# Two of seven column pairs by plain matmuls, and a new written order of steps

## The chip, the core and the metric

The kernel runs on one core of one Trainium2 chip. The core has a matrix engine (PE, with weight loads shown apart as PEld), a vector engine (DVE), a scalar engine (ACT), a general engine (POOL) and a queue engine (SP) that issues all transfers here. The metric is the device time of one execution in microseconds; lower is better.

## The reference

An input x of 2048 tokens by 512 is normalised by rows, and the result goes through two branches that are added to x. A is linear attention with 32 heads of 16 and a learned feature map; B is a gated unit without a nonlinearity.

```python
xn = _layernorm(x)
# A
qkv = (xn @ wqkv).reshape(B, S, 3, H, Dh)            # H = 32, Dh = 16
phi = [softmax(p @ w_phi), softmax(-p @ w_phi)]      # for q and for k, over the last axis
kv  = sum over tokens of phi_k * v;  z = sum over tokens of phi_k
o   = (phi_q @ kv) / (phi_q . z + 1e-6);  A = o @ wo
# B
B = ((xn @ w_gate) * (xn @ w_up)) @ w_down           # w_gate, w_up: 512 x 1792
out = x + A + B
```

## The kernel before

Tokens come in 16 tiles of 128, in four groups of four. Group 0 (tokens 0 to 511) is normalised at the start and transposed by PE. The other groups are normalised by steps s, sc and a, and transposed by a transfer on SP (step xt, line 523); group 1 (tokens 512 to 1023) lies in the tile x4, groups 2 and 3 in x16, as f16.

The gate and up product of group 0 is plain: for each of the 14 blocks of 128 columns a step g (4 matmuls of 512 columns with w_gate, line 351), a copy gc to SBUF, a step u (the same with w_up) and a step h, the product of both on DVE (line 371). For groups 1 to 3 the weights are scaled by a power of two in place (steps up, line 359), and columns k and k+7 form a pair, k from 0 to 6. A pair is multiplied with seven products of half-size blocks in place of eight (block_steps, from line 802): steps p1 to p7, 2 matmuls each, for gate (even b) and up (odd b), where b = 2k or 2k+1. Sums of weights (steps t) and of tokens (steps z for groups 2 and 3, Nz for group 1) are their inputs. Keeps k1 to k3 on ACT, joins j2, j7, j3 on DVE, a direct copy or product d, and for up the multiplications m on POOL or DVE make the hidden tile hT out of them. Groups 2 and 3 use matmuls of 512 columns. Group 1 has the same steps with an N in front and matmuls of 256 columns, with accumulators of its own (pool ps_f) that exist between the marks =f and =ab2 of the list.

The attention: steps vk or k (projection), kx and ky (exponentials, ACT), kr and ki (sum and reciprocal, DVE), kp (POOL, line 559) and kv (PE, sum over tokens, two accumulators that are masked by kvm0 and kvm1 at the end). For queries q, qx, qy, qr, qi, qp likewise, then the transposing transfer qt (line 616), ab (PE, line 627, one buffer of accumulators), de, rd, ot (DVE) and the transposing transfer oT (line 660). The folded weights come from steps fk and fq (line 471); fq waits for the transposing load wq.

The way out: for groups 0 and 1 and token tiles 8 and 12 steps f (w_down and wo, line 678), fs, and the store fo. Tiles 9 to 11 with 13 to 15 form three pairs n and m = n + 4, with seven products of half blocks again (pair_steps, steps P, K, A, B, J; sums S of hidden blocks and ct, cb, wt of w_down), and each tile's row is stored by one step X (line 1015).

The order of all this is written out as one list of words (ORDER): every word is a step, with /a, /v or /g for ACT, DVE or POOL where a step can run on more than one. Each engine runs its words in the order of the list; a second table (SLOTS) says which buffer of its ring each tile takes, six PSUM banks among them. Where a step with both inputs in SBUF goes to DVE, the next POOL step of the list is made to wait until it is over:

```python
        if on_pool and turn is not None:
            tc.add_manual_dep(on_pool[0], turn.name, AFTER, reason="turns")
            turn = None
        if on_dve and both_in_sbuf.match(name):
            turn = on_dve[-1]
```

Of the kernel before, what the change touches and what calls it, by code (L numbers as in the profile page):

```python
# [30 lines left out]
fqa0/v vk6.1 ky6 kv1 g2 fq2 kv2 kx6 kr4 ki4 kr6 ki6 fqv0/a fqv2/a kp4/g u5 kv3 vk7.0 vk7.1 kr5 kp6/g vc6/a gc2/a
n1.3 fqa2/a ky7 vk8.0 vk8.1 kv4 kx7 ki5 h5 u2 kr7 ki7 n1.4 kp5/g vc8/a kx8 ky8 a12/a vk10.0 vk10.1 vc7/a ky10
kx10 a13/a kp7/g h2 vk9.0 kv5 kr8 ki8 kp8/g kv6 xt12 vk9.1 ky9 vc10/a kx9 n0.4 q0.0 q0.1 a15/v kr10 vk11.0
vk11.1 ky11 ki10 kx11 kv7 kv8 vk12.0 q1.0 q1.1 kp10/g xt13 a14/v kr9 ki9 kp9/g vc11/a vc9/a xt14 Nz0/v qy0 qx0
kr11 ki11 qr0 qi0 g8 gc8/a qy1 u10 qx1 kp11/g n0.0 kv9 vk13.0 vk12.1 kv10 qr1 h10 xt15 ky12 kx12 qp0/g qi1
# [5 lines left out]
f2.6 f0.3 f2.5 f0.5 f1.1 qp3/g ot0 qx4 qy4 ab2 f1.8 qr4 up41/a qy7 qx7 qp6/g de2 qi4 f1.7 rd2 fs1 ot2 qt3 oT0
qp4/g q9.0 f3.5 q9.1 q8.0 q8.1 f0.2 qr7 z1/g inv0 ab3 qt6 oT2 up21/a de3 qi7 rd3 f3.3 ot3 qx9 qt4 t00/v t02/v
Nz1/v f0.8 up20/a qy9 qp7/g p1.1 f0.7 p1.0 qx8 qy8 k1.1/a Nz3/g k1.0/a ab5 de5/a up11/a f0.6 p2.0 f0.0 t01/v
p6.0 k2.0/a rd5 ot5 n2.5 up60/a f2.7 ab6 t03/g j2.0 f2.8 p7.0 de6/v k3.0/a oT3 f3.8 fs0 rd6 ot6 p2.1 p6.1 oT5
qt7 oT6 fs2 ab4 j2.1 fo2 z3/g de4/a rd4 ot4 k2.1/a q13.0 q13.1 qr8 p5.0 up10/a j7.0 t10/g Nz2/g p4.0 d4.0/a p7.1
Np2.1 ab7 de7/a f3.6 p5.1 f3.7 k3.1/a rd7 ot7 qy13 p4.1 p3.0 =f fs3 Np1.1 up31/a Nk1.1/a Np1.0 Nk1.0/a p2.3
Np6.1 qx13 j3.0 Np6.0 p2.2 Nj2.1 Nk2.1/a j7.1 d4.1 Nk2.0/a up30/a t11/g m2.1/g Np2.0 Nj2.0 t12/g p3.1 j3.1 Np7.0
Np7.1 Nk3.1/a Nk3.0/a p1.2 k1.2/a p1.3 qr9 m7.1/g Np4.1 Np4.0 Nd4.0/a p5.2 t13/v Np5.0 up40/a Nd4.1 p6.2 Nj7.0
Np5.1 j2.2 Np3.0 k2.2/a p5.3 m3.1/g t20/g k1.3/a Nj3.0 Nj7.1 j2.3 Nm2.1/g p7.2 Np2.2 k3.2/a Np1.2 Nk1.2/a p6.3
Np3.1 t21/g p4.2 Np6.2 j7.2 p3.2 p1.4 Nj3.1 k2.3/a Nj2.2 Nm3.1/v t22/v m2.3/g S0.0/g Nk2.2/a d4.2/a k1.4/a Np7.2  # L50
Nk3.2/a j3.2 p2.4 j2.4 p7.3 Np5.2 Np4.2 p2.5 p2.6 k3.3/a Nd4.2/a qi8 j7.3 n2.0 qp8/g Nj7.2 Nm7.1/g p1.5 Np1.3
Nk1.3/a qr13 p3.3 Np3.2 k1.5/a Nj3.2 Np6.3 p6.4 p6.5 Nk2.3/a Np7.3 j2.5 m2.5/g k2.4/a m7.3/v j3.3 Np5.3 Nk3.3/a
up50/a Nj7.3 p7.4 Np2.3 Np4.3 Nd4.3 p5.4 Np3.3 Nm7.3/g Nj2.3 k3.4/a Np1.4 Nk1.4/a p4.3 j7.4 Np2.4 Np6.4 k2.5/a
t23/g Nj3.3 qi13 t30/g Nm2.3/g Nk2.4/a p3.4 j3.4 p7.5 Np7.4 Np1.5 Nj2.4 n2.1 p4.4 d4.3 Nm3.3/v Nk3.4/a t31/v
Np2.5 q10.0 Np4.4 m3.3/g k3.5/a Nk1.5/a p5.5 p4.5 Np6.5 Nj2.5 qi9 j7.5 Nm2.5/g t32/g d4.4/a Nd4.4/a Np5.4 Nj7.4
p1.6 Nk2.5/a Np7.5 Nk3.5/a q10.1 t33/v d4.5 Np3.4 wr2 Nj3.4 wf2 k1.6/a p3.5 Np4.5 up51/a Nd4.5 p6.6 Np1.6
Nk1.6/a Np2.6 qx10 j2.6 k2.6/a qp9/g j3.5 Np5.5 Nj7.5 m7.5/v m3.5/v t40/v t41/g q12.0 p5.6 Np6.6 q12.1 p7.6
Nk2.6/a Np3.5 Np7.6 Nj2.6 Nj3.5 qy10 wp2 qp13/g k3.6/a p1.7 p1.8 Nk3.6/a qx12 k1.7/a Np5.6 Np4.6 p2.7 j7.6 p3.6
p4.6 Nm7.5/g Nd4.6/a oT4 qr10 Nj7.6 Np1.7 qy12 p2.8 p6.7 Np3.6 k1.8/a Nk1.7/a j3.6 k2.7/a Np6.7 j2.7 Nk2.7/a
d4.6/a q14.0 q14.1 Np7.7 Nj3.6 j2.8 Np2.7 p7.7 Nk3.7/a qx14 Np2.9 Nm3.5/v m2.7/v t42/v Nj2.7 k3.7/a Np4.7 qy14  # L60
Np5.7 Nd4.7 p5.7 Nj7.7 t43/g Np2.8 Np1.8 p4.7 Np3.7 j7.7 Nm2.7/g Nm7.7/v Nj3.7 Nm3.7/v Nk1.8/a Np6.8 Nk2.8/a
p1.9 d4.7 p3.7 k1.9/a Np7.8 Np5.8 p6.8 m7.7/g qt13 fo3 qt8 j3.7 p2.9 Nk3.8/a Np4.8 Nd4.8/a k2.8/a p1.10 Nj7.8
Nj2.8 Np3.8 m3.7/g Np1.9 j2.9 Nk1.9/a k1.10/a t50/v ws2 Nj3.8 S1.0/g p6.9 p2.10 Nj2.9 j2.10 Np6.9 p7.8 Np5.9
p5.8 k2.9/a m2.9/v p7.9 Nk2.9/a t52/v k3.8/a j7.8 Np7.9 Nk3.9/a t51/g p5.9 p1.11 p4.8 Nj7.9 p3.8 k3.9/a p4.9
t53/g p6.10 Np4.9 Np3.9 Nm2.9/v j7.9 d4.8/a j3.8 m7.9/g qi10 k1.11/a Nd4.9 p6.11 p3.9 Nj3.9 up61/a t60/v d4.9
Nm7.9/g qp10/g k2.10/a Np1.11 p2.11 j3.9 p7.10 k2.11/a k3.10/a j2.11 Np1.10 p5.10 j7.10 Nm3.9/g m2.11/g m3.9/v
Np2.10 Np2.11 Nk1.10/a Nj2.10 p4.10 p7.11 k3.11/a q15.0 q15.1 S0.3/v qy15 Nk1.11/a d4.10/v p4.11 p3.10 p5.11
Np6.10 qx15 Nk2.10/a p1.12 Nj2.11 Nm2.11/g j3.10 Np6.11 j7.11 t61/g t62/g t63/g Np2.12 Np7.10 p2.12 f6.3 d4.11
m7.11/g k1.12/a oT7 j2.12 Nk3.10/a Np4.10 Nk2.11/a Nd4.10/a f6.1 p3.11 f6.4 qr12 Np7.11 Np5.10 p1.13 ct2.2/a
Nk3.11/a Nj7.10 j3.11 p6.12 fo1 Np3.10 k2.12/a f7.0 Np4.11 k1.13/a p2.13 Nj3.10 S0.5/v j2.13 f7.4 Np1.12 f7.1  # L70
p7.12 cb11.1/a p6.13 Nk1.12/v Nd4.11 Np5.11 f6.8 qi12 Nj7.11 Nj2.12 S1.3/g S2.4/g m3.11/v k3.12/a S0.4/g S1.4/g
Np6.12 q11.0 f6.7 Nk2.12/a ct2.1/a Np7.12 Np3.11 p5.12 qr14 Nj3.11 Nk3.12/a j7.12 Nm3.11/g qp12/g Np4.12 p4.12
Np1.13 q11.1 p3.12 d4.12/a Nd4.12/a m2.13/v Nk1.13/a Np2.13 f7.2 Np5.12 f6.2 Np6.13 f7.8 k2.13/a qr15 j3.12
p7.13 Nj2.13 Nk2.13/a ct1.0/a qi14 Nj7.12 inv1 cb11.0/v qx11 k3.13/a p5.13 Np7.13 f4.2 f4.5 Np3.12 f4.1 Nk3.13/a
p4.13 wt1.0/v Nm2.13/v Nj3.12 Nm7.11/v Np5.13 f7.7 f6.0 qt9 Np4.13 j7.13 qp14/g Nj7.13 Np3.13 d4.13 Nd4.13 p3.13
f4.3 Nj3.13 =ab2 ab8 qy11 ct2.3/g S0.1/v de8/v rd8 ot8 qi15 f4.7 f6.5 f5.2 Nm3.13/g f4.4 f5.0 ct2.0/g ab9 f7.5
S0.2/v Nm7.13/v S2.6/g de9/a rd9 ot9 S2.2/v S2.3/v F12.3 f6.6 f4.8 F12.1 f7.6 wt2.0/v S1.1/g S1.5/g qt14 qt10
qp15/g qt12 m7.13/v oT8 f4.0 j3.13 f7.3 f4.6 F12.2 f5.8 fs4 fs6 ab14 f5.7 de14/a ct1.1/a rd14 oT9 fo0 ot14
S0.6/v m3.13/v f5.1 f5.4 qr11 qi11 f8.8 oT14 f12.5 F12.6 f8.3 fs7 f5.5 f5.3 F12.5 f12.2 ab12 f8.2 P1b.10 de12/a
wt1.1/g wt2.2/g P1a.10 f5.6 f8.7 cb21.0/a f8.5 f8.4 F12.0 K1.10/v S2.1/v rd12 ot12 f12.6 qt15 fo6 P1a.11 f12.1  # L80
# [1030 lines left out]
```

## Time and profile before

| | us |
|---|---|
| median of 3 runs | 214.34 (214.32 to 215.28) |
| profiled execution | 215.05 |
| its span, first to last instruction | 213.3 |
| PE busy | 206.5 (97%), 1452 matmuls |
| DVE busy | 185.3 (87%) |
| ACT busy | 153.2 (72%) |
| POOL busy | 149.8 (70%) |
| share of the chain that ended last | PE 78%, DMA 9%, DVE 6% |
| mean granted clock of PE | 0.998 |

The span covers the instructions; the time of an execution has 1.7 us more around it. Busy PE time is a union of matmuls whose ends are modelled, so the distance between starts says more of a matmul's price than its length. A wait line reads: who waited, for what, us in total, times, longest.

### The profile page before, as it was taken

How to read it: one execution, taken by the hardware profiler on the slowest of the kernel's cores; microseconds unless marked ns; L12 is line 12 of the kernel's file. 1: busy time of each engine (PE TensorE's matmuls, PEld its weight loads, DVE VectorE, ACT ScalarE, POOL GpSimd, SP SyncE). 2: the span in 40 equal slices, each digit the busy share in tenths (PEclk: the TensorE clock that was granted, in tenths of full speed). 3: DMA queues.
4: the chain of work that ended last, by engine and by line, in shares of the span. 5: the costliest groups of instructions: out<-in, count | busy, mean ns of one | idle time of the engine just before them, and what ended most of it. 6: DMA issues, size and time to landing. Idle time of an engine off the chain costs nothing.

```text
span 213.3 us, 4174 instructions
## 1 busy us (share of the span) xinstructions
PE 206.5 (97%) x1452; PEld 117.8 (55%) x1452; DVE 185.3 (87%) x372; ACT 153.2 (72%) x296; POOL 149.8 (70%) x146
## 2 busy tenths in 40 slices
...
GB/s 158 260 274 383 379 297 177 92 8 33 70 25 77 0 68 105 147 103 77 0 3 0 0 3 32 179 13 3 0 0 0 0 130 119 101 148 75 50 78 74
DMA packets 47253, 19.95 MB, mean 94 GB/s; under 512 B 37504, under 2 KB 46976, under 8 KB 47104
## 3 DMA queue, kind: packets, MB, share of 16 engines
q1 hardware_dynamic: 47232, 19.69, 40.6%
...
HBM read 8.67 MB, written 2.10 MB: 50 GB/s over the span
## 4 chain that ended last, share of the span: by engine, by line
PE 78%; DMA 9%; DVE 6%; SPq 2%; ACT 1%; POOL 1%; issue 1%; DVEq 0%; ACTq 0%; POOLq 0%
PE sa L824 16%; PE fin L678 15%; PE sc L824 9%; PE k L337 5%; PE q L337 5%; PE da L960 5%; PE pv L337 4%; PE sb L824 4%; DMA wT<-in_A_wqkv_dram 3%; PE u L351 3%; DMA wgu<-in_B_w_up_dram 2%; PE g L351 2%; DMA oT<-otok 2%; PE db L960 2%; PE dd L960 2%; PE dc L960 2%
## 5 line engine op out<-in xcount | busy, mean ns | idle before, releaser
L549 DVE TENSOR_REDUCE sums<-e 128x64 f32<-128x1024 f32 x32 | 38.3, 1198 | 3.0 <-ACT e L537 2.9
L559 POOL TENSOR_TENSOR phik<-e,rs 128x1024 bf16<-128x1024 f32 x16 | 30.8, 1935 | 13.8 <-DVE rs L554 10.4
L678 PE MATMUL fin<-wd,hT 128*128 128x512 bf16 (+2 forms) x154 | 37.1, 359 | 0.0
L559 POOL TENSOR_TENSOR phiq<-e,rs 128x1024 bf16<-128x1024 f32 x16 | 31.5, 1975 | 4.8 <-DVE hT L846 2.7
L824 PEld LDWEIGHTS <-T 128*128 128x128 f16 x224 | 21.9, 98 | 17.4 <-issue 0.5
L846 POOL TENSOR_TENSOR hT<-u_sb,hT 128x256 f16<-128x256 bf16 (+1 forms) x23 | 21.1, 920 | 5.3 <-DVE T L774 3.0
L357 ACT COPY k<-sa 128x512 f32<-128x512 f32 (+1 forms) x42 | 19.5, 483 | 5.6 <-PE sa L824 4.1
L359 ACT ACTIVATE k<-sa 128x512 f32<-128x512 f32 (+1 forms) x41 | 19.7, 494 | 4.9 <-PE sa L824 4.2
L824 PEld LDWEIGHTS <-wgu 128*128 128x128 bf16 x168 | 16.3, 98 | 12.3
L337 PEld LDWEIGHTS <-x 128*128 128x128 f16 x144 | 13.4, 98 | 14.4 <-DMA x<-xn 1.1
L678 PEld LDWEIGHTS <-hT 128*128 128x128 f16 (+1 forms) x154 | 14.0, 98 | 11.8
L337 PE MATMUL pv<-vk,x 128*128 128x512 bf16 x48 | 18.2, 379 | 0.8 <-DMA x<-xn 0.8
L351 PEld LDWEIGHTS <-wgu 128*128 128x128 bf16 x128 | 12.0, 98 | 12.0 <-DMA wgu<-in_B_w_up_dram 0.4
L554 DVE RECIPROCAL rs<-sums 128x64 f32<-128x64 f32 x32 | 17.3, 543 | 1.5
L337 PE MATMUL k<-vk,x 128*128 128x512 bf16 x48 | 18.2, 379 | 0.0
L824 PE MATMUL sa<-ss,T 128*128 128x512 f16 x56 | 16.3, 379 | 0.0
L839 DVE SCALAR_TENSOR_TENSOR hT<-sc,k 128x512 f16<-128x512 f32 (+1 forms) x28 | 15.3, 548 | 1.1 <-PE sc L824 0.9
L359 ACT ACTIVATE wgu<-wgu,up 128x1024 bf16<-128x1024 bf16 x14 | 16.0, 1152 | 0.0
L710 ACT ACTIVATE junk<-wgu 128x1024 bf16<-128x1024 bf16 x14 | 15.0, 1077 | 1.2 <-DMA wgu<-in_B_w_gate_dram 1.2
L843 DVE TENSOR_TENSOR u_sb<-sc,k 128x512 bf16<-128x512 f32 (+1 forms) x28 | 15.0, 545 | 0.6 <-PE sc L824 0.5
L537 ACT ACTIVATE e<-q 128x512 f32<-128x512 f32 x24 | 13.9, 601 | 1.9 <-POOL phik L559 1.4
L351 PE MATMUL u<-xnT,wgu 128*128 128x512 bf16 (+1 forms) x64 | 14.6, 352 | 0.1
...
## 6 DMA issues: line engine op xcount, KB each, us to landing
out_dram<-o_sb SPq DMA_DIRECT2D x15, 128.0 KB, 1.9
...
xall<-in_A_x_dram SPq DMA_DIRECT2D x1, 1024.0 KB, 12.1
xall<-in_A_x_dram SPq DMA_DIRECT2D x4, 128.0 KB, 2.5
...
```

Source lines behind the costliest of these rows:

```text
L337: nc.tensor.matmul(ps, lhsT=xt(n)[:, j, :], rhs=w[:, j, :], start=(j == 0), stop=(j == DC - 1))
L351: nc.tensor.matmul(ps, lhsT=w[:, c, f * P:(f + 1) * P], rhs=xnT[:, c, lo:hi], start=(c == 0), stop=(c == DC - 1))
L357: A.copy(out=dst, in_=src)
L359: A.activation(out=dst, in_=src, func=AF.Identity, scale=scale)
L549: V.tensor_reduce(out=sums[:], in_=ev(), axis=AX.X, op=ALU.add)
L554: V.reciprocal(out=rs[:].rearrange("p a b -> p (a b)"), in_=held.pop((s + "s", n))[:])
L559: eng.tensor_tensor(out=phi[:].rearrange("p g (x f) -> p (g x) f", f=DH), in0=ev(), in1=held.pop((s + "i", n))[:].to_broadcast((P, 2 * H, ...
L678: nc.tensor.matmul(held["fin", n, lo], lhsT=l, rhs=r, start=len(done) == 1, stop=len(done) == FC + DC)
L824: nc.tensor.matmul(mine[bankname], lhsT=ww[:, j, :], rhs=xx[:, j, :], start=start and j == 0, stop=(j == hc - 1), skip_group_check=True)
L839: V.scalar_tensor_tensor(out=h(*to), in0=mine[ps], scalar=gate_scale, in1=mine[kept][:], op0=ALU.mult, op1=ALU.add)
L846: eng.tensor_tensor(out=h(*to), in0=mine["u", i][:], in1=h(*to), op=ALU.mult)
L960: nc.tensor.matmul(mine[ps][:, 0:W], lhsT=l, rhs=r, start=bool(mine.pop((ps, "new"), False)), stop=True, skip_group_check=True)
```

## The change

Three things change.

Of the seven column pairs of group 1, the first five (KN = 5) keep the seven products of half blocks; pairs 5 and 6 are computed by the plain steps g, gc, u and h, as group 0 is, on the scaled weights and with x4 as the moving operand. These are units 19, 20, 26 and 27. The gate copy then has the factor that undoes the scaling. Groups 2 and 3 keep all seven pairs, so their weight sums t stay.

In the three pairs of token tiles at the end, the row of the second tile m (13, 14, 15) is stored in two halves of 256 columns, steps X13.0, X13.1 and so on, each after its own join.

The list ORDER and the table SLOTS are written anew in whole: steps move in order, and some to another engine.

```diff
     def half(w, name, T, f, lo, hi):
         ps = bank(name)[:, 0:hi - lo]
         for c in range(DC):
-            nc.tensor.matmul(ps, lhsT=w[:, c, f * P:(f + 1) * P], rhs=xnT[:, c, lo:hi],
+            nc.tensor.matmul(ps, lhsT=w[:, c, f * P:(f + 1) * P], rhs=(x4 if T else xnT)[:, c, lo:hi],
                              start=(c == 0), stop=(c == DC - 1))
...
-    def gate_copy(ps, n, eng=A):
+    def gate_copy(ps, n, eng=A, scale=None):
         g_sb = ring(gpool, "g", [P, TT], BF16, "g_sb")
-        copy(eng, g_sb[:, 0:n], ps)
+        copy(eng, g_sb[:, 0:n], ps, scale)
...
+    KN = 5
+    levels = (8.0, 8.0, 4096.0)
+    hidden_scale = 16.0
+    gate_scale = hidden_scale / (levels[0] * levels[1])
...
-            held["gc", u] = gate_copy(held.pop(("g", u)), TT - lo, eng)
+            held["gc", u] = gate_copy(held.pop(("g", u)), TT - lo, eng, gate_scale if T else None)
...
-    for u in range(FC):
+    for u in [*range(FC), *(FC + k + i for i in (0, FH) for k in range(KN, FH))]:
         unit_steps(u)
...
     for b in range(2 * FH):
         block_steps(b, 0)
-        block_steps(b, 1)
+        if b < 2 * KN:
+            block_steps(b, 1)
...
-        for t in (n, m):
-            steps[f"X{t}"] = (lambda t=t: nc.sync.dma_start(out=out_view(t, t + 1)[:, 0, :], in_=mine["o", t][:]), None)
+        def store(t, lo, hi):
+            nc.sync.dma_start(out=out_view(t, t + 1)[:, 0, lo:hi], in_=mine["o", t][:, lo:hi])
+
+        steps[f"X{n}"] = (lambda: store(n, 0, D), None)
+        for c in range(2):
+            steps[f"X{m}.{c}"] = (lambda c=c: store(m, c * W, (c + 1) * W), None)
```

Of the list, the start, the stretch behind kv15 and the end, old and new (other lines are left out):

```diff
-g3 gc3/a =k g1 gc1/a fk2 fk0 g0 u3 fkv2/v fkv0/v fka2/a fka0/a k1 ky1 kx1 u0 gc0/v h3 k0 u1 k2 h0 kr1 h1 ki1 kx0
...
-gc5/a a7/a vc5/a s13 h12 kx5 vk4.0 vk4.1 vc4/a kp3/g vk6.0 s14 fq0 xt10 s15 s12 sc12 xt8 xt9 xt7 ky4 kx4 ky5
...
-kp13/g z0/v n0.2 kx14 ky14 n1.5 kr14 q3.0 q5.0 kv12 vc15/a ki14 ky15 kx15 kp14/g qt1 q2.0 kr15 ki15 n1.1 kp15/g
-f3.1 q2.1 qx2 q3.1 f3.2 kv13 q5.1 f3.4 qy2 f3.0 f2.1 f2.0 qr2 qi2 qp2/g vc14/a kv14 f1.2 f1.3 f2.4 z2/v qx5 n2.2
-qy5 n1.2 kv15 qx3 qy3 kvm0 kvm1 =ab qr5 q4.0 f1.0 f1.6 ab1 n2.6 wr0 f2.2 de1 wf0 qt2 rd1 qi5 ot1 wp0 q6.0 q6.1
...
-P3a.9 P4a.11 P2b.10 de11/a rd11 ot11 X14 oT11 J3.9 X9 B6.10/g P3a.11 P4b.11 P2w.10 P4w.11 P5b.11 X13 P2a.10
-P3w.10 J2.10 K5.11/a P3b.10 A7.11/v B6.11/g J4.11 A1.11/v P3w.11 P8w.11 J8.11 X15 P3b.11 J3.11 P2b.11 P3a.10
-J3.10 X10 P2a.11 P2w.11 J2.11 X11
...
+g1 gc1/a g0 gc0/v =k u0 fk2 h0 fk0 fkv2/a fkv0/v fka0/a u3 g3 fka2/a k0 gc3/a u1 h1 h3 ky0 kx0 kr0 ki0 k2 k1 g2
...
+h13 xt5 xt6 kv0 kv1 g11 gc11/a u10 g9 g12 s13 h10 ki3 n1.4 sc8 a8/a gc9/a gc12/a kv2 vk4.0 vk4.1 wq vk5.0 a7/g
+xt7 vk5.1 ky4 kx4 a10/g a9/g a11/a kp3/g vk6.0 vc4/a vk6.1 s15 s12 s14 u12 ky5 kx5 vc5/a vc6/a kx6 ky6 sc12 kr4
...
+kr14 ki14 n0.5 kp14/g vk15.1 q3.0 q6.0 q2.1 kx15 ky15 kv12 vc15/a kr15 ki15 qx2 qy2 kp15/g q3.1 q4.0 q4.1 q5.0
+q5.1 kv13 f3.5 kv14 q6.1 f1.6 f1.0 f1.5 qr2 qi2 qy5 qx5 kv15 qr5 qi5 f0.0 f0.3 f0.5 kvm0 kvm1 =ab ab1 f0.4 n1.2
+qx3 qy3 f0.1 q7.0 qp2/g qt2 f1.4 qr3 f0.6 de1 rd1 n0.2 qi3 ot1 qy6 qp5/g qx6 q7.1 n1.6 ab0 wr0 qr6 qp3/g oT1 de0
+f0.2 f3.3 wf0 rd0 wp0 qi6 ot0 qt3 z0/v f2.3 ws0 f3.2 f3.0 n2.4 qy4 qx4 n2.6 qy7 qx7 f1.2 f2.5 ab2 qp6/g z1/g
+f2.6 f1.7 q8.0 f1.1 qt5 de2 qr7 rd2 ot2 n2.1 qr4 f1.8 q8.1 f2.0 ab3 up01/a up31/a de3 oT0 qi4 qp4/g f2.2 p1.1
+f0.7 up00/a inv0 f2.4 rd3 f0.8 f3.4 f3.6 k1.1/a qi7 ot3 fs0 z2/v t02/v t00/v ab5 z3/v n2.5 up21/a qy8 oT2 qt6
+oT3 p1.0 f2.7 t01/v k1.0/a de5/a qx8 f2.1 rd5 ot5 f1.3 f3.1 f2.8 qp7/g up11/a fo0 qt4 p6.1 p2.1 fs1 ab6 p6.0
...
+f5.8 Np1.9 k1.10/v m2.9/g cb11.0/a m7.7/v Nk2.8/a k2.9/a p7.9 Np7.8 Nk1.9/a j2.10 qr10 Nj2.9 g26 m3.7/g Nk3.8/a
...
+P3a.9 P2a.10 P8w.11 P2w.10 A7.9/g J4.9 K6.11/a P2a.11 P3b.9 J8.9 P3w.9 A6.10/v B6.10/v P2b.10 P2b.11 X13.1 X13.0
+X14.1 J3.9 A6.11/g B6.11/v X14.0 A1.11/v X9 P7a.11 P3b.11 P3w.10 P2w.11 P3w.11 J2.11 P7b.11 P3a.11 P3a.10 J2.10
+J3.11 P3b.10 X11 J3.10 X10 K7.11/a P4w.11 A7.11/g J8.11 X15.1 P4a.11 P4b.11 J4.11 X15.0
```

More of the change, by code (lines that the diff above doesn't have):

```diff
@@ L25 @@
 ORDER = """
-g3 gc3/a =k g1 gc1/a fk2 fk0 g0 u3 fkv2/v fkv0/v fka2/a fka0/a k1 ky1 kx1 u0 gc0/v h3 k0 u1 k2 h0 kr1 h1 ki1 kx0
-ky0 kr0 s6 s5 ky2 n1.0 g4 g6 gc4/a u6 g7 n0.5 kx2 gc6/a gc7/a s7 k3 kp1/g s4 sc4 kx3 n1.6 n0.6 ky3 u7 h7 h6 a5/g
-xt5 u4 g12 g11 g13 h4 ki0 u12 g9 u13 a6/g kp0/g gc11/a s9 s11 s10 s8 u11 a4/a xt4 n0.3 gc9/a kr2 gc13/a n0.1 h11
-h13 xt6 wq g10 gc10/a gc12/a kr3 n2.4 u9 h9 ki2 kv0 g5 sc8 a11/g a10/g vk5.0 a8/g xt11 ki3 vk5.1 kp2/g a9/a
-gc5/a a7/a vc5/a s13 h12 kx5 vk4.0 vk4.1 vc4/a kp3/g vk6.0 s14 fq0 xt10 s15 s12 sc12 xt8 xt9 xt7 ky4 kx4 ky5
@@ L31 @@
[L31 to L35, printed above, removed]
@@ L41 @@
[L41 to L45, printed above, removed]
@@ L46 @@
[L46 to L80, printed above, removed]
@@ new lines @@
+g7 g4 ky2 kx2 kx1 n0.0 gc7/a kr2 gc4/a s6 kp0/g g6 n0.6 ky1 gc6/a s4 s5 n0.4 s7 sc4 a4/g u6 kr1 n1.3 u2 u4 h4 h6
+ki2 ki1 k3 g13 a6/a gc13/a u7 g10 s8 s10 h7 s9 gc2/a a5/a ky3 u13 u9 xt4 gc10/a kp1/g kp2/g s11 kx3 h2 n0.3 kr3
+h13 xt5 xt6 kv0 kv1 g11 gc11/a u10 g9 g12 s13 h10 ki3 n1.4 sc8 a8/a gc9/a gc12/a kv2 vk4.0 vk4.1 wq vk5.0 a7/g
+xt7 vk5.1 ky4 kx4 a10/g a9/g a11/a kp3/g vk6.0 vc4/a vk6.1 s15 s12 s14 u12 ky5 kx5 vc5/a vc6/a kx6 ky6 sc12 kr4
+h9 ki4 n1.0 kp4/g a15/g h12 kr5 kv3 fq2 u11 h11 fqv2/a xt11 ki5 kr6 ki6 vk7.0 vk7.1 xt10 kp5/g xt8 fqa2/a fq0
@@ new lines @@
+kx7 ky7 fqa0/a vc7/a a13/a kv4 vk8.0 vk8.1 kr7 ki7 g5 gc5/v kp6/g kx8 ky8 vc8/a a12/a xt9 vk10.0 vk10.1 kv5 ky10
+xt12 kx10 kp7/g vc10/a a14/a kr8 ki8 kp8/g xt15 fqv0/v vk9.0 kr10 ki10 kv6 vk9.1 vk11.0 vk11.1 ky9 kx9 vc9/a
+kp10/g kr9 ki9 ky11 kx11 q0.0 q0.1 xt13 kv7 vc11/a q1.0 g8 q1.1 kp9/g kv8 vk12.0 u8 kv9 kv10 vk12.1 kr11 ki11
+qx0 qy0 qr0 gc8/v kp11/g xt14 n1.1 vk13.0 vk13.1 qx1 qy1 n0.1 ky12 qi0 qp0/g qt0 kv11 kx12 vc12/a h8 vc13/a qr1
+qi1 kr12 ki12 ky13 kx13 n1.5 kr13 ki13 q2.0 vk14.0 vk14.1 u5 h5 vk15.0 qp1/g qt1 kp12/g kp13/g vc14/a ky14 kx14
@@ new lines @@
+f0.7 up00/a inv0 f2.4 rd3 f0.8 f3.4 f3.6 k1.1/a qi7 ot3 fs0 z2/v t02/v t00/v ab5 z3/v n2.5 up21/a qy8 oT2 qt6
+oT3 p1.0 f2.7 t01/v k1.0/a de5/a qx8 f2.1 rd5 ot5 f1.3 f3.1 f2.8 qp7/g up11/a fo0 qt4 p6.1 p2.1 fs1 ab6 p6.0
+p2.0 k2.1/a de6/a j2.1 Nz0/g oT5 k2.0/a up20/a qt7 rd6 p7.1 f3.8 f3.7 k3.1/a up10/a p5.0 t03/g j2.0 ot6 fs3 ab4
+Nz1/g de4/v p7.0 p4.1 q9.0 fs2 p1.2 rd4 ot4 oT6 k3.0/a t10/g t11/g p4.0 up51/a d4.0/a ab7 j7.0 q9.1 p2.2 p5.1
+k1.2/a Nz2/g Nz3/g m2.1/g t12/g de7/v rd7 ot7 t13/g =f j7.1 p3.0 Np1.1 up30/a Nk1.1/a Np1.0 p6.2 j2.2 Np6.1
@@ new lines @@
+Nk1.0/a Np2.0 Np6.0 p3.1 d4.1 Np2.1 j3.0 qx9 Nj2.0 Nj2.1 Nk2.0/a Np7.0 p5.2 q10.0 Np2.2 up40/a Nk3.0/v j3.1
+Nk2.1/a Np7.1 Np4.0 k2.2/a q10.1 Nk3.1/a Np4.1 qr8 Nd4.0/a p7.2 Np5.0 Nd4.1 Nm2.1/v Np5.1 Nj7.0 m3.1/g t22/g
+p1.3 Nj7.1 up41/a Np3.0 qi8 qy9 Np2.3 Np3.1 k3.2/a k1.3/a p4.2 Nj3.0 Nj3.1 Np1.2 p6.3 qy10 j7.2 Nk1.2/a Np1.3
+Nm7.1/v t20/v k2.3/a t21/g p3.2 Nj2.2 Nk1.3/a j3.2 Np6.2 Nj2.3 Nk2.2/a m7.1/v p7.3 Nm3.1/v p5.3 Np7.2 k3.3/a
+j7.3 qr9 Nk3.2/a Np6.3 p2.4 q13.0 Np4.2 qp8/g qx10 Nk2.3/a Nd4.2/a d4.2/a p3.3 j3.3 Np7.3 q13.1 Np5.2 p1.4 p2.3
```

71 lines of the change are left out of this document (45 added, 26 removed).

## The prediction

> **What bounds the kernel now.** I read the page's busy shares first, then what the matrix engine waits for.
>
> ```profile
> PE 206.5 (97%) x1452; PEld 117.8 (55%) x1452; DVE 185.3 (87%) x372; ACT 153.2 (72%) x296; POOL 149.8 (70%) x146
> ```
> ```profile
> PE pv L337 <- DMA x<-xn: 0.8, 1, 0.8
> PE warm L377 <- PEq L1095: 0.8, 1, 0.8
> PE fin L678 <- DMA oT<-otok: 0.7, 1, 0.7
> PE kv L590 <- POOL phik L559: 0.6, 2, 0.4
> PE pq L471 <- DMA wT<-in_A_wqkv_dram: 0.3, 1, 0.3
> ```
>
> PE is busy all the time, and its visible waits are 3.2 us. A change can win only by removing PE work, by removing these waits, or in the tail after the last matmul. Next I read the busy time by stretch (columns: stretch, then us busy on PE, PEld, DVE, ACT, POOL, and the clock).
>
> ```profile
> 75.00:95.00 20.00, 19.27 (x131) 9.23 (x130) 18.23 (x40) 19.69 (x32) 17.92 (x14) 1.00 0.60 103
> 95.00:120.00 25.00, 24.96 (x163) 14.61 (x161) 24.40 (x48) 22.79 (x47) 21.92 (x20) 1.00 0.11 25
> 120.00:150.00 30.00, 30.00 (x181) 17.44 (x180) 28.80 (x68) 23.19 (x50) 22.13 (x21) 1.00 0.19 41
> ```
>
> From 75 to 150 us the vector engine is nearly as full as PE: a wait removed ahead of 75 need not survive the stretch behind it.
>
> For the size of a matmul I took the chain (start, us, what):
>
> ```profile
> 95.96 0.86 PE q L337 x4
> 101.73 0.44 PE sa L824 x4
> ```
>
> Four matmuls of 512 columns take 0.86 us (0.2158 each over a longer run), four of 256 take 0.44 (0.108 each). Adding these up in the order of the list gives the PE work ahead of every step; its start in the trace less that sum is how late PE runs. The first step, g3, starts at 11.74 with nothing ahead. Lateness grows by 0.46 at the fold fq0 (38.34 us), 1.04 at vk7.0 (43.51), 0.96 at kv14 and kv15 (72.5 and 74.4), 1.8 from there to 107 us (0.9 of it at f3.8), and 0.8 in small steps to the end: from 11.74 to 17.1, 5.4 in all.
>
> **The change, part by part.**
>
> *Plain matmuls.* For two column pairs, 4 blocks x 14 matmuls of 256 columns go (56 x 0.108 = 6.05 us) and 8 units x 4 of 512 come (32 x 0.2158 = 6.90). PE gets **+0.85**; nothing hides it, because PE is the full engine. Beside it, per pair: 6 keeps at 0.38 and one 0.39 copy leave ACT, two gate copies at 0.58 come (-1.5); 6 joins at 0.415 and one product at 0.42 leave DVE, two at 0.63 come (-1.65); three multiplications leave POOL (0.69) or DVE (0.28). Whole new list, with steps that change engine: ACT 146.7 to 141.7, POOL 143.9 to 141.3, DVE 177.1 to 178.0. DVE gets no lighter in all, only elsewhere: between PE work 96 and 130 its listed work falls from 34.3 to 30.1. PE shows no wait there, so that earns **0** (-0.4 for the gaps of 0.1 to 0.2 around 105, to +0.8 for a handover the new order makes tight).
>
> *The order up to kv15.* Three waits lose their cause. The transpose xt7 was ninth in SP's queue and is now fifth, behind xt4, xt5, xt6 and wq at 1.2 to 2.9 us of issue each; in the trace the fifth goes out at 34.85, and a7 (POOL 0.77) is listed behind sc8 and a8, so about 35. With 2.9 us to landing it is there at 38, and vk7.0 comes at about 41.6. The fold fq0 moves 5.4 us of PE work later, while wT landed at 38.3. And z0 leaves the place in front of the last two key reductions:
>
> ```profile
> 66.50 2.10 DVE L796 TENSOR_TENSOR ss<-x 128x1024 f16<-128x1024 f16 x1
> 73.76 1.16 DVE L796 TENSOR_TENSOR ss<-x 128x1024 f16<-128x1024 f16 x1
> ```
> ```profile
> 70.55 3.83 POOL L559 TENSOR_TENSOR phik<-e,rs 128x1024 bf16<-128x1024 f32 x2 [2.50 <-PE q L337]
> 74.33 2.38 POOL L559 TENSOR_TENSOR phiq<-e,rs 128x1024 bf16<-128x1024 f32 x1
> ```
>
> POOL stood 2.50 us in front of kp14 for that. Without z0, kr14 and kr15 can start when their exponents are there (65.9 and 68.4), and kp15 ends about 71 to 72, when PE work 59.5 brings kv15. The three are worth 0.46 + 1.04 + 0.96 = 2.46. In return the early gate and up units hand PSUM banks on more tightly: by these durations g10, u13, g11, u10 and fq0 find their bank free only 0.2 to 0.7 us ahead, and the trace has one such handover that cost 0.16 (u4). I take **-2.0**; ends 0 (new waits eat it) and -2.5.
>
> *The first attention half.* z0, z2 and z3 now lie on DVE between kvm0 and ot4, where before none of them lay (z2 came just ahead, z3 was on POOL). The accumulator ab has one buffer, so each ab waits for the ot before it. DVE's busy time from kvm0 to the end of ot4 was 21.4 us and took 22.9 (74.8 to 97.7): 1.5 of waits. In the new list it is 23.4 with the three at 1.16. With the same waits and the 0.5 to 0.6 from ot4 to ab7, ab7 comes 25.3 after kv15 and PE has 22.8 of work for that: 2.5 of standing where there was 1.4. I take **+1.0**. Ends: 0 (steps that nothing waits for slip behind) and +2.9 (each z at 2.10). The transposes oT2, oT3 and qt7 share SP with fo0, which now stands in front of qt4; at 2.4 to 3.2 us from issue to landing, f3.8 has 1 to 3 us where it was 0.7 short.
>
> Of the two rows of z I take 1.16, since the list holds the next POOL step until each is over and only the POOL step already running can overlap. The row beside it: z0 took 2.10 while POOL ran kp13, and qp2 took 2.38 instead of 1.94 while DVE ran z2. [...]
>
> *The second attention half.* With five pairs the narrow products end earlier, and ab8 moves from PE work 154.0 to 143.6. qp14 to ab14 shrinks from 7.7 to 6.0 us of PE work, for POOL 1.98, issue 1.23 and 3.2 to landing; the rest has more room. **+0.1** (0 to +1.0).
>
> *The tail.* The last store carries 64 KB for 128.
>
> ```profile
> out_dram<-o_sb SPq DMA_DIRECT2D x15, 128.0 KB, 1.9
> out_dram<-o_sb SPq DMA_DIRECT2D x1, 32.0 KB, 1.7
> ```
> ```profile
> 210.15 0.48 DVE L989 SCALAR_TENSOR_TENSOR o_sb<-db,inv,dK 128x256 bf16<-128x256 f32 x1 [0.39 <-PE db L960]
> ```
>
> Last matmul, join (0.48) and issue (0.34) stay as they are; K7.11, A7.11 and J8.11 (0.47, 0.72, 0.48) fit beside the seven matmuls of P4. Three more issues on SP lie ahead of the last, 0.34 each, in stretches where SP waits. **-0.15** (-0.4 to 0).
>
> Sum: 0.85 - 2.0 + 1.0 + 0 + 0.1 - 0.15 = -0.2. The profiled execution took 215.05 us (span 213.3 and 1.7 around it), 0.7 above the median of 214.34; it would take 214.85, and the median becomes **214.1**.
>
> **The rivals.**
>
> *The early saving comes through (faster).* If DVE's waits in the first attention half shrink, because xt7, the keys and the queries all come earlier, the third term is 0 to +0.3 and the first stretch gives 2.4: 0.85 - 2.4 + 0.15 - 0.2 = -1.6, **212.7**. For it: 1.5 us of DVE waits that could go, and 4.2 us less DVE work behind. Against: DVE was busy 91% of 75 to 95 already.
>
> *The z steps and POOL hold each other (slower).* Place: kvm0 to ab7. Price: 2.10 in place of 1.16 three times, 2.8 us on the engine that paces ab, so **216.9**; from about 1.5 us a step the kernel is slower by more than it can be told from no change. For it: the row of 2.10. Against: z2's row, and the held POOL steps. [...]
>
> *A transpose or store comes late in a new place (slower).* The SP queue is rewritten, and one step behind a waiting one stops those behind it: fo0 ahead of qt4, qt10 and qt13 ahead of qt9. One such wait cost 0.9 at f3.8 and 1.04 at vk7.0; two of them with the early saving kept at 1.5 give **216.0**. Against: most landings have 1 to 5 us of room.
>
> **How the numbers follow.** About 0.5% (1.07 us) is what a measurement of this kernel can tell from no change. The forecast gets 0.40 (213.3 to 215.3), the faster rival 0.30, the z rival 0.17, the late landing 0.13. The range reaches from the lower ends (0.85 - 2.5 - 0.4 - 0.4 with 0 for the third: -2.4) to a little above the z rival: 211.8 to 217.2.
>
> **What would show it.** PE's wait for x at vk7 and for phik at kv14 and kv15 are gone, kv15 starts near 72, and ab7 near 97; ss steps on DVE of about 1.2 us; no PE wait from 100 to 150; 24 fewer matmuls; the last store 1.8 us. Wrong if ab7 comes before 95.5 or after 98.5, if an ss row on DVE stands at 2.1, or if PE waits appear among the early gate and up units, where the trace of before has almost none.

## The result and the profile after

The changed kernel takes 212.44 us (median of 6, 212.35 to 212.55), the kernel before 214.63 in the same comparison (median of 6, 214.24 to 215.28). The ratio is 0.9896, with an interval of 0.9877 to 0.9915: faster by 1.0%. The number lies inside the range, but the likeliest case was "about the same" (214.1). What came is the first rival, the early saving that comes through (212.7).

The page's busy shares of the kernel after, and then all that PE waited for by the profile (us in total, times, longest):

```profile
PE 206.5 (98%) x1428; PEld 116.2 (55%) x1428; DVE 182.3 (87%) x367; ACT 148.1 (70%) x278; POOL 145.5 (69%) x143
```
```profile
PE warm L373 <- PEq L1097: 0.8, 1, 0.8
```

There are 24 matmuls fewer for 0.85 us more of work, and of the five wait lines of before only the start-up one is left. The same stretches as before, with the same columns:

```profile
75.00:95.00 20.00, 20.00 (x135) 9.74 (x134) 18.90 (x40) 19.65 (x32) 16.49 (x14) 1.00 0.66 114
95.00:120.00 25.00, 25.00 (x162) 15.04 (x162) 24.07 (x51) 22.58 (x48) 21.56 (x20) 1.00 0.11 22
120.00:150.00 30.00, 30.00 (x171) 16.39 (x169) 27.43 (x59) 20.08 (x39) 23.62 (x23) 1.00 0.02 5
```

From 75 to 95 VectorE (DVE) is even fuller than it was (18.90 for 18.23), and PE is full all the same. The steps z0, z2 and z3 now lie there; grouped by shape, in 70 to 96 us, they are these two rows (count, us in all, mean ns):

```profile
L793 DVE TENSOR_TENSOR ss<-x 128x1024 f16<-128x1024 f16 x2 | 1.4, 680 | 0.0
L793 DVE TENSOR_TENSOR ss<-x,ss 128x1024 f16<-128x1024 f16 x1 | 0.7, 684 | 0.0
```

Each took 0.68 us, where the rows of before were 1.16 and 2.10. The last key products on POOL (start, us):

```profile
66.38 1.94 POOL L559 TENSOR_TENSOR phik<-e,rs 128x1024 bf16<-128x1024 f32 x1 [0.44 <-DVE rs L554]
68.70 1.94 POOL L559 TENSOR_TENSOR phik<-e,rs 128x1024 bf16<-128x1024 f32 x1 [0.39 <-DVE rs L554]
```

POOL stands 0.4 us before each, no longer 2.50, and kp15 ends at 70.64, not at 74.37.

Lateness, the start of a step less the PE work ahead of it in the list, is counted as in the prediction. (Starts of narrow matmuls lie 0.109 us apart, not the 0.108 counted, so some 0.6 us of the growth behind ab7, before and after alike, is no standing.) Its growth by stretch tells where the time went:

| growth of lateness, us | before | after | difference |
|---|---|---|---|
| first step to kv15 | 2.71 | 0.37 | -2.34 |
| kv15 to ab7 | 1.41 | 0.37 | -1.04 |
| ab7 to the last matmul | 1.25 | 1.18 | -0.07 |
| PE work of the list | | | +0.85 |
| end of the last matmul to the end of the span | 3.23 | 3.13 | -0.10 |

The sum is -2.7, the difference of the spans (213.3 and 210.6). The medians differ by 2.2, because the profiled execution of before was 0.4 to 0.7 above its medians.

### The profile page after: what moved, and what is told of

It reads as the page before. It is cut to its first block, busy times and chain, and to the rows that moved or that the text cites. A ratio compares the mean times of both kernels' runs of the same rounds, so it can differ in the third digit from the quotient of the medians.

```text
span 210.6 us, 4089 instructions
## 1 busy us (share of the span) xinstructions
PE 206.5 (98%) x1428; PEld 116.2 (55%) x1428; DVE 182.3 (87%) x367; ACT 148.1 (70%) x278; POOL 145.5 (69%) x143
## 4 chain that ended last, share of the span: by engine, by line
PE 98%; DVE 0%; ACT 0%; issue 0%
PE fin L678 18%; PE sa L821 16%; PE sc L821 8%; PE u L347 8%; PE g L347 7%; PE pv L333 7%; PE q L333 7%; PE k L333 7%; PE da L958 5%; PE sb L821 4%; PE ab L627 2%; PE kv L590 2%; PE warm L373 2%; PE dc L958 2%; PE db L958 2%; PE dd L958 2%
## 5 line engine op out<-in xcount | busy, mean ns | idle before, releaser
L559 POOL TENSOR_TENSOR phiq<-e,rs 128x1024 bf16<-128x1024 f32 x16 | 30.9, 1934 | 13.8 <-ACT dK L355 5.4
L821 PEld LDWEIGHTS <-T 128*128 128x128 f16 x192 | 18.4, 98 | 14.1 <-issue 0.2
L347 PEld LDWEIGHTS <-wgu 128*128 128x128 bf16 x160 | 15.4, 98 | 14.7 <-issue 0.2
L355 ACT ACTIVATE k<-sa 128x512 f32<-128x512 f32 (+1 forms) x33 | 16.8, 515 | 7.2 <-PE sa L821 5.7
L843 POOL TENSOR_TENSOR hT<-u_sb,hT 128x512 f16<-128x512 bf16 (+1 forms) x19 | 17.9, 952 | 4.3 <-DVE hT L843 3.0
L821 PEld LDWEIGHTS <-wgu 128*128 128x128 bf16 x144 | 14.0, 97 | 12.1 <-DVE otok L654 0.2
L353 ACT COPY k<-sa 128x512 f32<-128x512 f32 (+1 forms) x33 | 16.6, 508 | 4.7 <-PE sa L821 3.1
L771 POOL TENSOR_TENSOR T<-wgu,T 128x512 f16<-128x512 bf16 x11 | 12.8, 1159 | 5.1 <-DVE T L771 4.2
L840 DVE TENSOR_TENSOR u_sb<-sc,k 128x512 bf16<-128x512 f32 (+1 forms) x24 | 13.7, 575 | 2.4 <-PE sc L821 1.7
L367 DVE TENSOR_TENSOR hT<-u,g_sb 128x512 bf16<-128x512 f32 (+2 forms) x20 | 12.3, 625 | 3.7 <-PE u L347 3.5
```

What stands on the lines that cost most here:

```text
L347: nc.tensor.matmul(ps, lhsT=w[:, c, f * P:(f + 1) * P], rhs=(x4 if T else xnT)[:, c, lo:hi], start=(c == 0), stop=(c == DC - 1))
L353: A.copy(out=dst, in_=src)
L355: A.activation(out=dst, in_=src, func=AF.Identity, scale=scale)
L559: eng.tensor_tensor(out=phi[:].rearrange("p g (x f) -> p (g x) f", f=DH), in0=ev(), in1=held.pop((s + "i", n))[:].to_broadcast((P, 2 * H, ...
L821: nc.tensor.matmul(mine[bankname], lhsT=ww[:, j, :], rhs=xx[:, j, :], start=start and j == 0, stop=(j == hc - 1), skip_group_check=True)
L843: eng.tensor_tensor(out=h(*to), in0=mine["u", i][:], in1=h(*to), op=ALU.mult)
```

## The experiments

Each ratio is to the kernel before, run on the same chip in the same comparison; it is not exactly the quotient of the two medians. Some 20 matmul records are missing in the traces of experiments 1 to 8, so steps were matched to records by tile and size. All growths, in us:

| | ratio (interval) | to kv15 | to ab7 | to the end |
|---|---|---|---|---|
| before | 1 | 2.71 | 1.41 | 1.25 |
| after | 0.9896 (0.9877 to 0.9915) | 0.37 | 0.37 | 1.18 |
| 1, old list, xt7 early | 0.9939 (0.9918 to 0.9959) | 1.64 | 0.66 | 1.30 |
| 2, as 1, and z0 late | 0.9941 (0.9907 to 0.9976) | 0.31 | 1.44 | 1.52 |
| 6, as 2, and f3.8 later | 0.9951 (0.9928 to 0.9973) | 0.41 | 1.09 | 1.58 |
| 4, new list, z0 back | 0.9949 (0.9926 to 0.9972) | 1.11 | 0.61 | 1.18 |
| 8, new list, z doubled | 0.9963 (0.9947 to 0.9979) | 0.37 | 1.52 | 1.18 |
| 7, new list, POOL not held | 1.0168 (1.0101 to 1.0234) | 0.37 | 6.57 | 1.19 |
| 3, old list, plain pairs | 1.0206 (1.0175 to 1.0236) | 2.28 | 0.66 | 5.61 |
| 5, as 3, spread out | 1.0308 (1.027 to 1.0346) | 3.07 | 0.67 | 6.37 |
| 9, as 5, h later | 1.0073 (1.0047 to 1.0098) | 1.83 | 1.38 | 2.31 |
| 10, new list, whole stores | 0.9899 (0.9875 to 0.9922) | 0.37 | 0.38 | 1.17 |

### 1. The old list with xt7 early

```diff
-... gc5/a a7/a vc5/a s13 ... xt10 s15 s12 sc12 xt8 xt9 xt7 ky4
+... gc5/a a7/a xt7 vc5/a s13 ... xt10 s15 s12 sc12 xt8 xt9 ky4
```

> The kernel before with one step moved: the transpose xt7 goes out sixth instead of ninth in SP's queue. Theory (PE is full behind, so an early wait that goes is kept to the end): the wait of 0.85 us for x at vk7.0 is gone, kv15 starts near 73.4 instead of 74.4, and the time falls by 0.8 to 1.1 us. Rival (the vector engine paces 75 to 100 us and takes the saving back): kv15 near 73.4 all the same, but ab7 still near 98 and the time within 0.3 us of before.

Measured: 213.57 for 214.87, ratio 0.9939. Of the growth to kv15 1.07 is gone, and vk7.0 waits no longer; the price of that wait (1.04) was right. By the ratios this one word, moved, brings 0.6 of the 1.0 per cent of the whole change.

### 2. As 1, and z0 behind wp0

```diff
-kp13/g z0/v n0.2 kx14 ... ot1 wp0 q6.0
+kp13/g n0.2 kx14 ... ot1 wp0 z0/v q6.0
```

> The kernel before with xt7 sixth in SP's queue and z0 moved from in front of kr14 to behind wp0. Theory: kp14 and kp15 no longer wait for z0, kv15 starts near 72.5, z0 costs the vector engine 0.7 to 1.2 us between kvm0 and ot4, where PE had 1.4 us of standing; the time falls by 1.2 to 1.9 us. Rival (vector engine takes it back): no more than 1.0 us, the same as with xt7 alone.

Measured: 213.18 for 214.87, ratio 0.9941. By the ratio that is nothing on top of experiment 1, by the medians 0.4 us, and the interval leaves both open; a fall of 1.3 to 1.7 us also lies inside the theory's 1.2 to 1.9, so the times alone don't decide. The trace says more. kv15 comes with a growth of only 0.31, 1.33 less than in experiment 1, but most of that is given back, and most of it at one step in the first attention half. PE's waits:

```profile
PE fin L700 <- DMA oT<-otok: 0.9, 1, 0.9
PE warm L395 <- PEq L1118: 0.8, 1, 0.8
```

That is f3.8, 1.09 us late, waiting for the transposing transfer oT3. So a loss of the size of the term "first attention half, +1.0" does exist in the old list, but at a transfer and not at ab.

### 3. The old list with pairs 5 and 6 plain

The narrow steps of blocks 10 to 13 go, and the eight units (g and u of 19, 20, 26 and 27) come in their place, 12.5 us of PE work from the start of the first to that of the last, each copy gc and each product h right behind its unit:

```diff
-m3.9/v Np2.10 Np2.11 Nk1.10/a Nj2.10 p4.10 ... p5.11 Np6.10 qx15 Nk2.10/a p1.12
+m3.9/v g19 gc19/a u19 h19 p4.10 ... p5.11 g26 gc26/a qx15 p1.12
...
```

> The kernel before with only column pairs 5 and 6 of tokens 512 to 1023 by the plain steps, set at the places of the steps that they replace; nothing else moves. Theory (PE is full there, so only its work counts): 0.8 to 0.9 us slower. Rival (the lighter vector and scalar engine pay for it): within 0.3 us of before. If a handover of a bank goes wrong at the new places: 1.5 us slower or more, with a wait of PE between 145 and 160 us to show it.

Measured: 219.28, ratio 1.0206: +4.4 us, where the work alone is +0.85. That is the third of the cases expected. PE's waits in 140 to 178 us:

```profile
PE fin L697 <- DVE hT L386: 0.9, 1, 0.9
PE sc L840 <- DVE hT L855: 0.8, 1, 0.8
PE sb L840 <- ACT g_sb L374: 0.7, 1, 0.7
PE sa L840 <- ACT g_sb L374: 0.7, 1, 0.7
PE u L366 <- ACT g_sb L374: 0.3, 1, 0.3
```

Five late handovers behind the units, none of which the changed kernel shows.

### 4. The changed kernel with z0 back in front of kr14

```diff
-vc14/a ky14 kx14 kr14 ki14 n0.5 kp14/g vk15.1 q3.0 ... ot0 qt3 z0/v f2.3
+vc14/a ky14 kx14 n0.5 vk15.1 z0/v kr14 ki14 kp14/g q3.0 ... ot0 qt3 f2.3
```

> The changed kernel with z0 put back in front of kr14 and kr15. Theory: kp15 ends 1.0 to 1.5 us later than 70.6, so kv15 starts at 71.9 to 72.4 instead of 71.65; the vector engine is 0.7 us lighter behind kvm0; the time is 0.1 to 0.6 us longer than that of the changed kernel (212.44). Rival (z0 is as long as in the kernel before, 2.10, and holds up both key reductions): 1.0 to 1.5 us longer.

Measured: 213.39, ratio 0.9949, so half of the gain is gone. That is 0.95 more than 212.44, above the theory's 0.1 to 0.6 and just under the rival's 1.0. The span is 211.6 for 210.6: 0.74 of the loss comes before kv15, 0.24 between kv15 and ab7, and nothing is given back after that. In the new list z0's place is worth 1.0 us; in the old one the growths of experiments 1 and 2 differ by 0.3 in all (3.60 and 3.27), which the times don't resolve. POOL's key products kp12 and kp13, and z0 beside them (start, us):

```profile
62.17 3.82 POOL L578 TENSOR_TENSOR phik<-e,rs 128x1024 bf16<-128x1024 f32 x2
```
```profile
65.52 1.02 DVE L812 TENSOR_TENSOR ss<-x 128x1024 f16<-128x1024 f16 x1 [1.03 <-PE k L352]
```

POOL ends at 65.99 and z0 at 66.54, 0.55 later. The two rows of before read the same way: kp13 ended at 68.05 and z0 at 68.59; kp15 at 74.37 and z2 at 74.92. Neither 1.16 nor 2.10 was the price of the step; both were 0.55 plus what POOL had left.

### 5. As 3, with the units spread out

```diff
-m3.9/v g19 gc19/a u19 h19 p4.10 p7.11 ... p5.11 g26 gc26/a qx15 p1.12 j3.10 u26 h26
+m3.9/v g19 p4.10 gc19/a p7.11 ... p5.11 u19 qx15 p1.12 h19 j3.10 ...
...
```

> The list of before, with pairs 5 and 6 of tokens 512 to 1023 plain as in the run before, but the eight units now spread over 17 us of PE work instead of 8.4. Theory (work is 0.85, the rest is placement): the five waits of 0.5 to 1.0 us behind the units shrink to 0 to 1.5 in all, so +0.9 to +2.3 us against before, ratio 1.004 to 1.011. Rival (each plain unit brings its handover wait wherever it stands): +3.4 us or more, ratio 1.016 or more.

Measured: 220.73, ratio 1.0308. The theory fell: more room between the units made it worse. (By the list, the first and the last unit start 19.0 us of PE work apart, for 12.5 in experiment 3 and 8.9 in the changed kernel; the 17 and 8.4 of the expectation don't come out of the lists.) The waits of VectorE in 140 to 176 us point to the reason:

```profile
DVE hT L386 <- PE u L366: 9.2, 4, 2.8
DVE u_sb L859 <- PE sb L840: 0.5, 1, 0.5
```

L386 is the step h. VectorE stood 9.2 us there, because in its written order h came one PE step behind its u; the joins listed behind h then came late for PE. In experiment 3 the same wait was 5.4 us. In the changed kernel, from 136 to 157 us, it is 0.3, although h26 stands right behind u26 there too: VectorE was still busy with the steps listed ahead when u was done. Ahead of kv15 this execution also lost 0.4 more than before (at the unit u4 and the fold fq0), in a part of the list that is as before; the edit does not explain that.

### 6. As 2, with f3.8 behind ab4

```diff
-k3.0/a oT3 f3.8 fs0 rd6 ot6 p2.1 p6.1 oT5 qt7 oT6 fs2 ab4 j2.1
+k3.0/a oT3 fs0 rd6 ot6 p2.1 p6.1 oT5 qt7 oT6 fs2 ab4 f3.8 j2.1
```

> The list of before with xt7 early and z0 late, as in the run that gave 0.9941, and f3.8 moved three units later, behind ab4. Theory (in the old list the saving of z0 is lost to the transfer of oT3 alone, which f3.8 waits for 1.09 us): the wait goes, ab7 starts about 95.1 instead of 96.2, and the ratio falls to 0.989 to 0.991. Rival (VectorE paces the accumulator ab): ot4 ends 0.3 earlier at most, the wait moves from f3.8 to ab7, and the ratio stays at 0.993 to 0.995.

Measured: 212.97, ratio 0.9951. The wait at f3.8 went, and ab4 and ab7 took it over (0.59 and 0.19 us in lateness); ab7 started at 95.53. PE's wait lines have in its place:

```profile
PE ab L649 <- DVE otok L676: 0.4, 1, 0.4
```

ot4 ends at 95.33 for 95.61 in experiment 2, in an execution whose first step came 0.41 earlier. That is the rival, with a ratio at its upper edge: in the old list VectorE's own pace stands right behind the transfer, and moving this one step doesn't get z0's saving through.

### 7. The changed kernel without the hold on POOL for z, t and ws

```diff
-    both_in_sbuf = re.compile(r"(N?z|t|wt|c[bt]|S|N?m|[AB]|a|ws)\d")
+    both_in_sbuf = re.compile(r"(Nz|wt|c[bt]|S|N?m|[AB]|a)\d")
```

> The changed kernel, but POOL's next step is no longer held back for the steps z, t and ws on VectorE. Theory (z took 0.68 us because no POOL step ran beside it): z0, z2 and z3 take 1.1 to 2.1 us each, POOL's steps beside them also get longer, ab7 comes 1 to 3 us later than 95.0, and the ratio to before is 0.994 to 1.003. Rival (z is short here for another reason): the three stay at 0.68, qp6 and qp7 start up to 1.5 us earlier, ab7 is at 95.0 or before, and the ratio is 0.990 or less.

The pattern also makes ws wait for the POOL step listed ahead of it; with ws out of the pattern that wait goes too.

Measured: 217.70, ratio 1.0168, worse than the theory's worst; ab7 comes at 101.46. On VectorE (start, us):

```profile
78.29 0.68 DVE L812 TENSOR_TENSOR ss<-x 128x1024 f16<-128x1024 f16 x1
78.89 1.90 DVE L753 TENSOR_SCALAR up<-up 128x2 int32<-128x2 int32 x1
80.82 2.05 DVE L754 TENSOR_SCALAR up<-up 128x2 f32<-128x2 f32 x1
...
90.38 2.01 DVE L812 TENSOR_TENSOR ss<-x 128x1024 f16<-128x1024 f16 x1
92.31 1.71 DVE L790 TENSOR_TENSOR T<-wgu 128x512 f16<-128x512 bf16 x2
```

and POOL in the same time:

```profile
78.39 2.37 POOL L578 TENSOR_TENSOR phiq<-e,rs 128x1024 bf16<-128x1024 f32 x1
80.72 2.12 POOL L812 TENSOR_TENSOR ss<-ss,x 128x1024 f16<-128x1024 f16 x1
...
89.90 1.93 POOL L578 TENSOR_TENSOR phiq<-e,rs 128x1024 bf16<-128x1024 f32 x1
91.79 1.60 POOL L812 TENSOR_TENSOR s<-x 128x512 f16<-128x512 f16 x1
```

z0 began 0.1 us ahead of POOL's step and took its 0.68; POOL's step took 2.37 instead of 1.94. Two steps of ws on two numbers a partition, 0.16 and 0.17 us in the changed kernel, took 1.90 and 2.05: they end at 80.79 and 82.87, 0.03 us behind POOL's two steps (80.76 and 82.84). z2 began behind qp7 and ended 0.56 after it. Of the three z steps only z2 was long; z3, at 93.94, took 0.68 as z0 did. So in these rows the step that began second was the long one: POOL's step is 0.43 us longer behind z0, and the small ones and z2 end 0.03 and 0.56 us behind POOL's steps. Why the two engines hold each other up the trace doesn't show.

PE paid for it in two waits:

```profile
PE ab L646 <- DVE otok L673: 2.4, 1, 2.4
PE sa L840 <- DVE T L790: 1.6, 1, 1.6
```

A third part is the clock. Behind the first wait the granted clock of PE was 0.66 over 5 us (third column from the end), and lateness grew by 1.7 there without a wait:

```profile
85.00:90.00 5.00, 4.53 (x21) 1.89 (x21) 3.53 (x8) 3.92 (x7) 2.53 (x4) 0.66 0.52 102
```

Two of the four executions, 218.80 (this one) and 218.77, have a mean clock of 0.992; the other two, 216.63 and 216.64, have 1.000 and 0.998. So without the dip of the clock the kernel is some 4 us slower than the changed one (212.44), with it some 6. That PE's standing brought the dip was not tried.

### 8. The changed kernel with z0, z2 and z3 done twice

```diff
-        eng.tensor_tensor(out=S[:, i], in0=a, in1=b, op=op)
+        for _ in range(2 if eng is V and not group else 1):
+            eng.tensor_tensor(out=S[:, i], in0=a, in1=b, op=op)
```

> The changed kernel, with z0, z2 and z3 each done twice on VectorE: 3 x 0.68 = 2.05 us more between kvm0 and ot4. Theory (VectorE paces ab between kvm0 and ot4, so each us on it there is a us of the kernel): ab7 comes at 96.9 to 97.1, the ratio to before is 0.997 to 1.000. Rival (the 1.13 us in which VectorE is idle there takes half of it up): ab7 at 95.9 to 96.1, ratio 0.993 to 0.995.

Measured: 213.45, ratio 0.9963. The added 2.05 us of VectorE cost 1.1 us, all of it between kv15 and ab7 (at 96.08, 1.07 later than in the changed kernel), and nothing is given back. That is the rival's half; the ratio lies between the two expectations. The loss did not fall where either theory had put it:

```profile
PE sa L841 <- DVE T L790: 0.8, 1, 0.8
```

The step p6.1 waits for t01, which stands behind z2, z3 and two more t steps in VectorE's order; ab7 is late only because PE is. The doubled z0 cost nothing: VectorE has 0.59 us idle behind ws0 in the changed kernel.

### 9. As 5, with h three to five PE steps behind u

```diff
-u19 qx15 p1.12 h19 j3.10 ... g26 f6.1 gc26/a p3.11 f6.4 qr12 u26 p1.13 h26 ct2.2/a
+u19 p2.12 f6.3 d4.11 m7.11/g k1.12/a oT7 j2.12 g26 f6.1 h19 gc26/a p3.11 ...
...
```

> The list of before with the same two pairs plain; the eight units spread over 22 us of PE work, the gate copy one PE step behind its unit and the product h three to five PE steps behind its unit u, where it stood right behind u in the two runs before (VectorE stood 9.2 us there waiting for u). Theory (VectorE standing at h in its written order makes the PE waits): VectorE waits less than 3 us for u, the PE waits between Np1.9 and ab8 fall from 4.5 to 1.5 us or less, ratio to before 1.004 to 1.012. Rival (the six PSUM banks leave no room for whole units beside the blocks in this list): the waits stay at 3 us or more, ratio 1.016 or more.

Measured: 216.03, ratio 1.0073. VectorE's wait for u, from 136 to 176 us, and PE's two wait lines from 136 to 178:

```profile
DVE hT L386 <- PE u L366: 0.4, 1, 0.4
```
```profile
PE sa L840 <- ACT k L374: 0.3, 1, 0.3
PE fin L697 <- ACT g_sb L374: 0.3, 1, 0.3
```

From Np1.9 to ab8 lateness grows by 1.17, where it was 4.5 in experiment 5. The theory holds: with h further back VectorE's wait for u and most of PE's waits of experiment 5 are gone. (The units also stand over 22 us for 19; but spreading alone had made it worse in experiment 5. Three of the five waits of experiment 3 were for gate copies on ACT; whether h held those up too is not shown.) What is left, +1.6 us, is the 0.85 of work and a few handovers.

### 10. The changed kernel with whole stores

```diff
-... X13.1 X13.0 X14.1 J3.9 ... X14.0 ... J8.11 X15.1 P4a.11 P4b.11 J4.11 X15.0
+... X13 J3.9 ... X14 ... J8.11 P4a.11 P4b.11 J4.11 X15
```

> The changed kernel with tiles 13, 14 and 15 stored whole, each at the place of its second half. Theory (the halved store is worth a little in the tail): from the last matmul to the end of the span 3.2 to 3.3 us instead of 3.1, ratio to before 0.990 to 0.991. Rival (the last store's time does not hang on its size, or the three more issues cost as much): tail 3.0 to 3.1 us, no difference.

Measured: 212.38, ratio 0.9899, not to be told from 0.9896. In the trace the last matmul ends 0.10 earlier with everything else, and the span ends where it did: 3.24 us behind the last matmul for 3.13. The stores of the changed kernel and of this one (size, median us to landing):

```profile
out_dram<-o_sb SPq DMA_DIRECT2D x12, 128.0 KB, 1.9
out_dram<-o_sb SPq DMA_DIRECT2D x6, 64.0 KB, 1.6
```
```profile
out_dram<-o_sb SPq DMA_DIRECT2D x15, 128.0 KB, 1.9
```

A halved last store is worth some 0.1 us in one trace; the times don't resolve it.

## Why the prediction was right or wrong

**Plain matmuls (+0.85): right for this list.** The work counts up to 0.85, and from ab7 to the end the growth is as it was (1.18 for 1.25), so the lighter VectorE and ACT earned nothing, as the "0" of the prediction says. Experiments 3, 5 and 9 show that the new handovers are not free by themselves: 0.7 us more in experiment 9 and up to 5.7 in experiment 5, above all by the place of h. The upper end of that term (+0.8) was far too low for a careless place, and the changed list avoids it.

**The order up to kv15 (-2.0): right, a little small.** It gave -2.34, and kv15 starts at 71.65. Of that, xt7 is about 1.1 (experiment 1), z0 0.74 to 1.3 (experiments 4 and 2), and the fold fq0 about 0.3, read from the lateness there alone (grown by 0.48 before, by 0.17 after); it was not tried by itself. The new waits among the early units, which the upper end of 0 stood for, did not come.

**The first attention half (+1.0): wrong; this step failed.** It gave -1.04, outside its ends of 0 and +2.9, and ab7 came at 95.01, below the bound of 95.5 that the prediction itself had set. The term was 23.4 us of VectorE work, 1.5 of idle and 0.5 from ot4 to ab7, against 22.8 of PE work. Measured were 21.58 (kvm0 to the end of ot4), 1.13 and 0.15, against 23.0, and 0.50 from kv15 to kvm0 that the term had left out. The largest part is the price of z: three times 0.68 instead of 1.16, 1.44 of the 1.8 by which the work was overrated. The base was misread too: between kvm0 (74.84) and the end of ot4 (97.66) in the kernel before, VectorE was busy for 20.96 us and idle for 1.86, not 21.4 and 1.5. The row of 1.16 was taken for the price of a z step under the hold; 0.48 us of it was the wait for kp15. The prediction had the mechanism (only the POOL step already running can overlap) and read the wrong price from it. At the three new places POOL ended within 0.2 us of the start. Experiment 8 shows that the other assumption, that each us on VectorE here is a us of PE, was too strong as well: of 2.05 us more on VectorE only 1.07 reached PE, through p6.1, so three z at 1.16 would by that proportion have cost some 0.75 (an estimate), not 1.44.

What the term was measured against was partly chance besides. Of the 1.41 before, 0.88 was f3.8 waiting for the transfer oT3. The same order of these steps showed that wait as 0.86 in experiment 9 and as none in 1, 3 and 5. In the changed kernel oT3 is issued at 85.10 and f3.8 comes 4.86 us behind the issue's end; in the old order f3.8 came 1.9 to 3.6 us behind it, and by the traces oT3 landed 1.3 to 3.5 us behind it. So the changed list has more than 1 us of room where the old one had none.

**The rivals.** The early saving came through, as the first rival says: 212.7 for 212.44. Its number is closer than its terms: it had 0 to +0.3 for the first attention half, where -1.04 came, and its sum of -1.6 stood on 214.34, where the kernel before now took 214.63. VectorE's idle time from kvm0 to ot4 shrank as that rival says, from 1.86 to 1.13 us. The z rival is real (experiment 7) and kept away by the hold on POOL's next step, which the prediction gave as the reason against it. Its three z steps of 2.10 came in no run: in the changed kernel each took 0.68, and without the hold z2 alone was long (2.01). Without the hold the kernel is some 4 us slower than with it even where the clock did not dip (216.63 and 216.64 for 212.44). PE waited for no transfer or store in a new place. Two of the prediction's numbers don't follow from its own terms: with each z at 2.10 the term of the first attention half is 1.0 + 2.8 = 3.8, as the z rival's 216.9 counts it, not 2.9; and the late landing's 216.0 is 216.6 with the forecast's other terms (0.85 - 1.5 + 1.0 + 0.1 - 0.15 + 0.9 + 1.04 on top of 214.34).

**The second half (+0.1) and the tail (-0.15): right.** From p1.9 to ab11 the growth is 0.56 for 0.47; the tail is 3.13 for 3.23.

**As a whole,** the sum of -0.2 missed the measured -2.2 (-2.7 in the profiled executions) by one term that was 2.0 too high and another that was 0.3 too high. That the old list lost most of z0's saving in the first half, in the traces of experiments 2 and 6, shows that the doubt was not idle. What it left out is that the new list has other PE work between kv15 and ab7 and issues oT3 ahead of qt4 on SP; what each of these is worth was not tried by itself.
